# Pooled attention into gated attention experts: single PSUM banks, all loads cast on the way, and one written order for four engines

## The chip, the core and the metric

The kernel runs on one core of a Trainium2 chip. The metric is the device time of one execution in microseconds, as the median of several runs. A core has five instruction streams that matter here: TensorE (PE; its weight loads are listed apart as PEld), VectorE (DVE), ScalarE (ACT), GpSimd (POOL) and the sync engine (SP), which only issues transfers. They run at the same time, each in its own fixed order, and wait for each other through semaphores.

## The reference

There are 8 batches of 576 rows, 8 heads of 64. Stage A is attention against pooled keys and values: each run of 8 rows of k and of v is averaged, so 576 queries see 72 keys per head. The result x (576 x 512) goes into stage B, four causal attention experts of width 64, of which each row uses its best two, weighted by a softmax over their gates:

```python
k_p = k.reshape(B, H, Sp, pool, D).mean(axis=3)
v_p = v.reshape(B, H, Sp, pool, D).mean(axis=3)
attn = softmax(q @ k_p.T / sqrt(D));  x = attn @ v_p
...
topk = np.argpartition(-(x @ w_gate), 2)[..., :2]
for e in range(E):
    a = softmax(causal((x @ wq[e]) @ (x @ wk[e]).T / sqrt(Hd)))
    ye = a @ (x @ wv[e]) @ wo[e]
    out += (weight of e where e is in topk) * ye
```

(The softmax and causal mask are shortened here.)

## The kernel before, in words

Work is cut into units, each a few matmuls and what takes their result out of PSUM. One letter names a unit and a number its batch, so `N3:5` is unit N, index 3, of batch 5.

- `L` loads one chunk of k, q or v (three, five and three chunks a batch) by a GpSimd transfer that casts fp32 to bf16 (line 105). Four raw buffers of each kind turn round, so loads run up to three batches ahead.
- `Pk`, `Pv` pool k and v by matmuls with a small averaging matrix (line 199). ACT takes k out, DVE takes v out.
- `Pt` transposes the pooled k, `Q` transposes two heads of q (line 236), both copied out by DVE.
- `E` makes A's scores of two heads (line 252) and their exponentials on ACT (line 259). The scores of two heads share a double bank of 2 x 512, and each ACTIVATE covers half of the queries of both heads.
- `N` multiplies them with the pooled v of one head (line 268). A column of ones in v gives the sum; DVE takes its reciprocal (276) and multiplies (277).
- `X` transposes x (288), copied out by DVE (293).
- `q`, `k` project for a pair of experts, half of the rows at a time (361); ACT copies all of them out (368).
- `v` projects v of all four experts and the gate logits for 128 rows (303). With the fifth block DVE computes the gates, eleven small steps in one run (`gates`, lines 323 to 348).
- `s` makes B's scores for a pair of experts (387), exponentials on ACT (397), and zeroes the diagonal blocks' upper half on GpSimd (404).
- `o` multiplies them with v (417, one expert, two parts), and DVE scales by sum and gate (427 to 432). `T` transposes that (442), `y` multiplies with wo (455), and DVE (even blocks) or ACT (odd blocks) copies out before the store (467, 465).

The order on TensorE and GpSimd is the string SEQ. The order on DVE and ACT is made by a scheduler from its own costs. PSUM holds eight banks: the pool `p2` has two slots of two banks for scores, and `p1` four slots of one bank for everything else. A slot is used again in turn, so a new tile waits until the tile so many places before it has been read.

At the start batch 0 and the weights come uncast through SP (lines 113 to 131) into staging tiles, and DVE casts them (114, 136 to 148). One-element copies on GpSimd (lines 150 to 154) hold the loads of batch 1 back until a chunk of batch 0's v has arrived.

Of the kernel before, what the change touches and what calls it, by code (L numbers as in the profile page):

```python
# [8 lines left out]
FP32 = mybir.dt.float32  # L9
# [10 lines left out]
def kernel(  # L20
# [12 lines left out]
    nc = tc.nc  # L33
# [15 lines left out]
    NRAW = 4  # L49

# [4 lines left out]
    p2 = ctx.enter_context(tc.tile_pool(name="p2", bufs=2, space=bass.MemoryType.PSUM))  # L55
    p1 = ctx.enter_context(tc.tile_pool(name="p1", bufs=4, space=bass.MemoryType.PSUM))
    apool = ctx.enter_context(tc.tile_pool(name="apool", bufs=2))
    qtp = ctx.enter_context(tc.tile_pool(name="qtp", bufs=4))
    xtmp = ctx.enter_context(tc.tile_pool(name="xtmp", bufs=2))
    osp = ctx.enter_context(tc.tile_pool(name="osp", bufs=2))  # L60
    ofp = ctx.enter_context(tc.tile_pool(name="ofp", bufs=4))
    gtp = ctx.enter_context(tc.tile_pool(name="gtp", bufs=2))
    stp = ctx.enter_context(tc.tile_pool(name="stp", bufs=1))

    ident = const.tile([128, 128], BF16, name="ident")
    make_identity(nc, ident[:])

    KR = 96
    SPP = 96
    pool4 = const.tile([KR, 32], BF16, name="pool4")  # L70
    nc.gpsimd.memset(pool4[:], 1.0 / POOLW)
    nc.gpsimd.affine_select(
        out=pool4[:], in_=pool4[:], compare_op=ISGE, fill=0.0, base=0,
        pattern=[[-4, 32]], channel_multiplier=1,
    )
    nc.gpsimd.affine_select(
        out=pool4[:], in_=pool4[:], compare_op=ISGE, fill=0.0, base=3,
        pattern=[[4, 32]], channel_multiplier=-1,
    )

    qraws, kraws, vraws = [], [], []
    for i in range(NRAW):
        qraws.append(const.tile([128, NTC, H, D], BF16, name=f"qraw{i}"))
        kraws.append(const.tile([KR, 3, H, 2, D], BF16, name=f"kraw{i}"))
        vraws.append(const.tile([KR, 3, H, 2, D], BF16, name=f"vraw{i}"))
        nc.gpsimd.memset(qraws[i][64:128, NTC - 1, :, :], 0.0)

    def chunk(kind: str, b: int, c: int, dst):
        if kind == "q":
            n = min(128, S - 128 * c)  # L90
            return dst[0:n, c, :, :], q[b, :, 128 * c : 128 * c + n, :].rearrange("h p d -> p h d")
        return (
            dst[:, c, :, :, :].rearrange("p h t d -> p h (t d)"),
            (k if kind == "k" else v)[b, :, 2 * KR * c : 2 * KR * (c + 1), :].rearrange(
                "h (p t) d -> p h (t d)", t=2
            ),
        )

    CHUNKS = [("k", c) for c in range(3)] + [("q", c) for c in range(NTC)] + [("v", c) for c in range(3)]
    RAWS = {"q": qraws, "k": kraws, "v": vraws}  # L100

    def load_cast(b: int, i: int):
        kind, c = CHUNKS[i]
        dst, src = chunk(kind, b, c, RAWS[kind][b % NRAW])
        nc.gpsimd.dma_start(out=dst, in_=src)  # L105

    stage = {}
    for kind, c in CHUNKS:
        if c == 0:
            shape = [128, NTC, H, D] if kind == "q" else [KR, 3, H, 2, D]  # L110
            stage[kind] = stp.tile(shape, FP32, name=f"st_{kind}", tag=f"st_{kind}")
        dst, src = chunk(kind, 0, c, stage[kind])
        nc.sync.dma_start(out=dst, in_=src)  # L113
        nc.vector.tensor_copy(out=chunk(kind, 0, c, RAWS[kind][0])[0], in_=dst)  # L114

    wst = {}
    for nm, src, tag in (("q", moe_wq, "st_k"), ("k", moe_wk, "st_q"), ("v", moe_wv, "st_v")):
        wst[nm] = stp.tile([128, E, NFC, HD], FP32, name=f"wst_{nm}", tag=tag)
        nc.sync.dma_start(
            out=wst[nm][:].rearrange("p e fc d -> p (e fc) d"),  # L120
            in_=src.rearrange("e (fc p) d -> p (e fc) d", p=128),
        )
    wst["g"] = stp.tile([128, NFC, E], FP32, name="wst_g")
    nc.sync.dma_start(
        out=wst["g"][:], in_=moe_w_gate[:, :].rearrange("(fc p) e -> p fc e", p=128)
    )
    wst["o"] = stp.tile([128, NEP, DM], FP32, name="wst_o")
    nc.sync.dma_start(
        out=wst["o"][:],
        in_=moe_wo.rearrange("e d n -> (e d) n").rearrange("(ep p) n -> p ep n", p=128),  # L130
    )
    wqk = {}
    for ep in range(NEP):
        for nm in ("q", "k"):
            wqk[nm, ep] = const.tile([128, NFC, 128], BF16, name=f"w{nm}p{ep}")
            nc.vector.tensor_copy(
                out=wqk[nm, ep][:].rearrange("p fc (e d) -> p e fc d", e=2),
                in_=wst[nm][:, 2 * ep : 2 * ep + 2, :, :],
            )
    wvg = const.tile([128, NFC, VG], BF16, name="wvg")  # L140
    nc.vector.tensor_copy(
        out=wvg[:, :, 0 : E * HD].rearrange("p fc (e d) -> p e fc d", e=E), in_=wst["v"][:]
    )
    nc.vector.tensor_copy(out=wvg[:, :, E * HD : VG], in_=wst["g"][:])
    wop = []
    for ep in range(NEP):
        wop.append(const.tile([128, DM], BF16, name=f"wop{ep}"))
        nc.vector.tensor_copy(out=wop[ep][:], in_=wst["o"][:, ep, :])

    for i in range(NTC):  # L150
        nc.gpsimd.tensor_copy(out=qraws[1][0:1, i, 0, 0:1], in_=stage["v"][0:1, 1, 0, 0, 0:1])
    for r in (kraws[1], vraws[1]):
        for i in range(3):
            nc.gpsimd.tensor_copy(out=r[0:1, i, 0, 0, 0:1], in_=stage["v"][0:1, 1, 0, 0, 0:1])

    NETA, NETB, NKT, NVA, NXT = 4, 3, 4, 2, 2
    etas = [const.tile([SPP, 2, SPAD], BF16, name=f"eta{i}") for i in range(NETA)]
    for t in etas:
        nc.vector.memset(t[:, :, S:SPAD], 1.0)
    EOFF = [0, 576, 1024, 1344, 1536]  # L160
    ECOLS = 1664
    etbs = [const.tile([128, 2, ECOLS], BF16, name=f"etb{i}") for i in range(NETB)]
    for t in etbs:
        nc.vector.memset(t[:, :, 1600:ECOLS], 1.0)
    kts = [const.tile([128, SPAD], BF16, name=f"kt{i}") for i in range(NKT)]
    for t in kts:
        nc.vector.memset(t[:, S:SPAD], 0.0)
    vaugs = [const.tile([128, NTC, E, HD + 1], BF16, name=f"vaug{i}") for i in range(NVA)]
    for t in vaugs:
        nc.vector.memset(t[:, :, :, HD : HD + 1], 1.0)  # L170
    ones = const.tile([KR, 1], BF16, name="ones")
    nc.vector.memset(ones[:], POOLW / 4.0)
    one_ps = p1.tile([SPP, 1], FP32, name="one_ps", tag="p1")
    for c in range(3):
        nc.tensor.matmul(
            out=one_ps[32 * c : 32 * c + 32, :], lhsT=pool4[:, :], rhs=ones[:], start=True, stop=True
        )
    vps = [const.tile([SPP, H, D + 1], BF16, name=f"vpaug{i}") for i in range(2)]
    for t in vps:
        for h in range(H):  # L180
            nc.vector.tensor_copy(out=t[:, h, D : D + 1], in_=one_ps[:])
    xTbufs = [const.tile([128, NFC, SPAD], BF16, name=f"xT{i}") for i in range(NXT)]
    oTbufs = [const.tile([128, SPAD], BF16, name=f"oT{i}") for i in range(4)]
    for t in xTbufs:
        nc.vector.memset(t[:, :, S:SPAD], 0.0)
    for t in oTbufs:
        nc.vector.memset(t[:, S:SPAD], 0.0)
    turn = {"eta": 0, "etb": 0, "kt": 0, "oT": 0}

    def take(kind, ring):  # L190
        t = ring[turn[kind] % len(ring)]
        turn[kind] += 1
        return t
# [51 lines left out]
    def scores_a(st, hp: int):  # L245
        eta = st["eta", hp] = take("eta", etas)
        qT, kpT = st["qT", hp], st["kpT"]
        for c0, c1 in ((0, S // 2), (S // 2, S)):
            s_ps = p2.tile([SPP, 2, 512], FP32, name="sA_ps", tag="p2")
            for hh in range(2):  # L250
                r0 = hh * D
                nc.tensor.matmul(  # L252
                    out=s_ps[:, hh, 0 : c1 - c0],
                    lhsT=kpT[r0 : r0 + D, hp, :],
                    rhs=qT[r0 : r0 + D, c0:c1],
                    start=True,
                    stop=True,
                )
            nc.scalar.activation(  # L259
                out=eta[:, :, c0:c1], in_=s_ps[:, :, 0 : c1 - c0], func=EXP, scale=ATT_EXP_SCALE  # L260
            )

    def av_a(st, h: int):
        eta, vpaug, x_tm = st["eta", h // 2], st["vp"], st["x_tm"]
        hh = h % 2
        o_ps = p1.tile([128, NTC, D + 1], FP32, name="oA_ps", tag="p1")
        for c in range(NTC):
            nc.tensor.matmul(  # L268
                out=o_ps[:, c, :],
                lhsT=eta[:, hh, c * 128 : (c + 1) * 128],  # L270
# [24 lines left out]
    def v_proj(st, tc_: int):  # L295
# [19 lines left out]
        if tc_ == NTC - 1:  # L315
            st["G"] = gates(L)

# [242 lines left out]
```

The softmax here doesn't subtract the row's maximum and nothing guards it: scores larger than these inputs give would overflow.

## Time and profile before

| what | before |
|---|---|
| time, median of 4 runs | 208.4 us (208.3 to 208.54) |
| span of the profiled execution | 206.8 us |
| PE busy | 176.1 us, 2133 matmuls |
| DVE busy | 157.4 us, 567 instructions |
| ACT busy | 123.7 us, 225 instructions |
| POOL busy | 96.7 us, 181 instructions |
| first projection starts | 34.8 us |
| transfers | 87404 packets, 73.5% of 16 engines' span from GpSimd, 25.1% from SP |

Busy time is the union of an engine's instructions, and matmuls are pipelined, so a full TensorE need not be at its peak. Slices are fortieths of the span, in tenths. A group of instructions has a line, an engine, output and inputs with shapes, a count, the busy time, the mean of one, and the idle time before it with what ended it. The chain follows the work back from the last instruction to what released each step.

### The profile page before, as it was taken

To read this page: it belongs to the slowest core of one execution; us is meant where nothing else is said; L and a number is where in the kernel's file an instruction comes from. 1 tells how busy PE (TensorE), PEld (TensorE's weight loads), DVE (VectorE), ACT (ScalarE), POOL (GpSimd) and SP (SyncE) were. 2 spreads that over 40 slices of the span, in tenths; PEclk is the share of its full clock that TensorE was granted. 3 is DMA by queue.
4 is the path that set the end of the run, shared out by engine and by line. 5 is a ranking of instruction groups with operands and counts; after the bars stand their busy time and mean duration, and the time that the engine had idled before them with its cause. 6 is when DMAs were issued, how large, how long until landed. Compare 5 with 4: busy or idle time off the path is not lost.

```text
span 206.8 us, 5590 instructions
## 1 busy us (share of the span) xinstructions
PE 176.1 (85%) x2133; PEld 117.0 (57%) x2147; DVE 157.4 (76%) x567; ACT 123.7 (60%) x225; POOL 96.7 (47%) x181
## 2 busy tenths in 40 slices
PE   0126779999999899989999999999998999999762
PEld 0001446665676577646865776667755776785530
DVE  4645685749977987998989869997998779968642
ACT  2000442599358956765788667685877597747611
POOL 6009849785973493572845673635113012303300
PEclk9999999999999999999999999999999999999955
DMA  6999999999899969699599997997222102204315
GB/s 167 273 274 200 184 224 169 173 172 136 59 156 196 149 87 164 103 179 202 47 146 169 131 148 78 249 122 66 28 101 79 54 0 103 82 3 152 129 44 187
DMA packets 87404, 27.84 MB, mean 135 GB/s; under 512 B 77904, under 2 KB 82512, under 8 KB 87376
## 3 DMA queue, kind: packets, MB, share of 16 engines
q0 software_dynamic: 65744, 12.39, 73.5%
q1 hardware_dynamic: 21632, 15.09, 25.1%
q8 instruction: 17, 0.28, 0.5%
q14 instruction: 11, 0.09, 0.2%
HBM read 30.42 MB, written 9.44 MB: 193 GB/s over the span
## 4 chain that ended last, share of the span: by engine, by line
PE 61%; DVE 12%; ACT 12%; issue 5%; SPq 4%; DMA 3%; POOL 0%; ACTq 0%; DVEq 0%; POOLq 0%
PE qp_ps L361 7%; PE vg_ps L303 7%; PE oB_ps L417 6%; PE y_ps L455 6%; PE kp_ps L361 5%; PE sA_ps L252 5%; PE qT_ps L236 4%; PE xT_ps L288 4%; SPq L113 4%; ACT etb L397 4%; ACT eta L259 4%; PE sB_ps L387 4%; PE oA_ps L268 4%; DMA st_v<-in_v_dram 3%; DVE x_tm L277 3%
## 5 line engine op out<-in xcount | busy, mean ns | idle before, releaser
L404 POOL TENSOR_SCALAR_AFFINE_SELECT etb<-etb 128x256 bf16<-128x256 bf16 (+1 forms) x80 | 29.2, 386 | 81.1 <-ACT etb L397 76.7
L397 ACT ACTIVATE etb<-sB_ps 128x1024 bf16<-128x1024 f32 x64 | 50.0, 846 | 9.1 <-PE sB_ps L387 8.7
L259 ACT ACTIVATE eta<-sA_ps 96x576 bf16<-96x576 f32 x64 | 38.2, 644 | 12.6 <-PE sA_ps L252 11.9
L105 POOL DMA_DIRECT2D qraw<-in_q_dram x35 | 30.6, 876 | 2.1 <-DMA kraw<-in_k_dram 1.6
L277 DVE TENSOR_TENSOR x_tm<-oA_ps,rz 128x320 bf16<-128x320 f32 x64 | 30.6, 485 | 1.1
L303 PE MATMUL vg_ps<-wvg,xT 128*128 128x260 bf16 x160 | 23.7, 274 | 0.2
L268 PE MATMUL oA_ps<-vpaug,eta 96*128 96x65 bf16 x320 | 21.6, 200 | 1.9 <-ACT eta L259 1.5
L455 PE MATMUL y_ps<-wop,oT 128*128 128x512 bf16 x66 | 22.1, 415 | 1.2 <-DVE xT L293 0.7
L236 PE MATMUL qT_ps<-ident,qraw 128*128 128x128 bf16 x160 | 15.9, 233 | 8.0 <-DVE qraw L114 7.9
L417 PE MATMUL oB_ps<-vaug,etb 128*128 128x65 bf16 x480 | 21.8, 193 | 0.9 <-POOL etb L404 0.7
L268 PEld LDWEIGHTS <-eta 96*128 96x128 bf16 x320 | 16.2, 100 | 10.4 <-issue 4.0
L361 PE MATMUL qp_ps<-xT,wqp 128*128 128x288 bf16 x128 | 21.6, 291 | 0.2
L417 PEld LDWEIGHTS <-etb 128*128 128x128 bf16 x480 | 18.7, 97 | 4.9 <-issue 2.5
L467 DVE COPY ofin<-y_ps 128x512 f32<-128x512 f32 (+1 forms) x24 | 16.3, 683 | 6.7 <-PE y_ps L455 4.3
L368 ACT CAST qTB<-qp_ps 128x288 bf16<-128x288 f32 x32 | 12.8, 401 | 13.6 <-PE qp_ps L361 13.1
L361 PE MATMUL kp_ps<-xT,wkp 128*128 128x288 bf16 x128 | 20.9, 286 | 0.1
L310 DVE CAST vaug<-vg_ps 128x256 bf16<-128x256 f32 x40 | 16.8, 422 | 5.3 <-PE vg_ps L303 4.8
L387 PE MATMUL sB_ps<-qTB,kt 64*128 64x512 bf16 (+2 forms) x192 | 18.2, 277 | 2.7 <-ACT etb L397 1.9
L368 ACT CAST kt<-kp_ps 128x288 bf16<-128x288 f32 x32 | 12.9, 402 | 9.9 <-PE kp_ps L361 9.5
L105 POOL DMA_DIRECT2D vraw<-in_v_dram x21 | 16.9, 811 | 3.3 <-DMA kraw<-in_k_dram 2.2
L211 ACT CAST kp<-kp_ps 96x512 bf16<-96x512 f32 x8 | 4.7, 584 | 22.6 <-PE kp_ps L199 22.6
L242 DVE COPY qT<-qT_ps 128x576 bf16<-128x576 bf16 x32 | 14.2, 452 | 4.6 <-PE qT_ps L236 4.5
(72 smaller groups left out, 280.9 us busy)
## 6 DMA issues: line engine op xcount, KB each, us to landing
out_dram<-ofin SPq DMA_DIRECT2D x32, 256.0 KB, 2.2
kraw<-in_k_dram POOLq DMA_DIRECT2D x21, 192.0 KB, 6.7
vraw<-in_v_dram POOLq DMA_DIRECT2D x21, 192.0 KB, 5.8
qraw<-in_q_dram POOLq DMA_DIRECT2D x28, 128.0 KB, 6.1
st_k<-in_k_dram SPq DMA_DIRECT2D x3, 384.0 KB, 4.6
st_v<-in_v_dram SPq DMA_DIRECT2D x3, 384.0 KB, 5.9
st_q<-in_q_dram SPq DMA_DIRECT2D x4, 256.0 KB, 4.9
out_dram<-ofin SPq DMA_DIRECT2D x8, 128.0 KB, 2.7
```

The costliest lines, as they stand in the source:

```text
L105: nc.gpsimd.dma_start(out=dst, in_=src)
L259: nc.scalar.activation(out=eta[:, :, c0:c1], in_=s_ps[:, :, 0 : c1 - c0], func=EXP, scale=ATT_EXP_SCALE)
L268: nc.tensor.matmul(out=o_ps[:, c, :], lhsT=eta[:, hh, c * 128 : (c + 1) * 128], rhs=vpaug[:, h, :], start=True, stop=True,)
L277: nc.vector.tensor_tensor(out=x_tm[:, :, h * D : (h + 1) * D], in0=o_ps[:, :, 0:D], in1=rz[:].to_broadcast([128, NTC, D]), op=MULT,)
L303: nc.tensor.matmul(out=vg_ps[:], lhsT=xT[:, fc, tc_ * 128 : (tc_ + 1) * 128], rhs=wvg[:, fc, :], start=(fc == 0), stop=(fc == NFC - 1),)
L361: nc.tensor.matmul(out=p_ps[:], lhsT=wqk[nm, ep][:, fc, :], rhs=xT[:, fc, cols], start=(fc == 0), stop=(fc == NFC - 1),)
L368: nc.scalar.copy(out=st[nm, ep][:, cols], in_=p_ps[:])
L387: nc.tensor.matmul(out=s_ps[:, e, off : off + c1 - c0], lhsT=kT[r0 : r0 + HD, kc * 128 : (kc + 1) * 128], rhs=qT[r0 : r0 + HD, c0:c1], sta ...
L397: nc.scalar.activation(out=et[:, :, eo : eo + off], in_=s_ps[:, :, 0:off], func=EXP, scale=MOE_EXP_SCALE)
L404: nc.gpsimd.affine_select(out=blk, in_=blk, pattern=[[0, 2], [1, n]], compare_op=ISGE, fill=0.0, base=0, channel_multiplier=-1,)
L417: nc.tensor.matmul(out=o_ps[:, qc, :], lhsT=et[:, eloc, col : col + 128], rhs=vaug[:, kc, e, :], start=(kc == 0), stop=(kc == qc),)
L455: nc.tensor.matmul(out=y_ps[:], lhsT=st["oT", ep][:, qc * 128 : (qc + 1) * 128], rhs=wop[ep][:], start=(ep == 0), stop=(ep == NEP - 1),)
```

## The change

The change rewrites how units use PSUM, how data come in, and who sets the order.

1. All PSUM tiles take one bank, from one pool of eight slots. Scores of two heads or two experts go to two tiles, with one ACTIVATE for each. The last 64 queries of all pairs are collected into a unit of their own (`E4`, `s2x`), so the others are 512 columns wide. N takes two heads, o two experts.
2. Batch 0 and the weights are loaded by casting GpSimd transfers too. Staging tiles, casts and the holding copies go. The constants are made after the first 13 loads, the weights come as 15 loads after load 30. Memsets of the padding go to DVE.
3. SEQ now sets the order on TensorE, ACT, DVE and GpSimd. A letter `d` sends a projection's or an output's copy to DVE, otherwise ACT makes it: of 64 projection copies 31 go to DVE, of 40 output copies 10.
4. The gates become nine units (`g0` to `g8`) that other work can stand between. DVE takes reciprocals and products of N and o in pairs.
5. There are three xT buffers in place of two, eight slots for qT and for output tiles in place of four. The scores' results are kept per batch, two of each.
6. The new order puts stage A of batches 0 and 1 and much of 2 before the first projection, and works on two or three batches at a time up to the end.

The purpose is to have more PSUM tiles under way, to share the copies between ACT and DVE, to keep dependent small steps apart, and to free DVE of the casts.

```diff
-    p2 = ctx.enter_context(tc.tile_pool(name="p2", bufs=2, space=bass.MemoryType.PSUM))
-    p1 = ctx.enter_context(tc.tile_pool(name="p1", bufs=4, space=bass.MemoryType.PSUM))
+    p1 = ctx.enter_context(tc.tile_pool(name="p1", bufs=8, space=bass.MemoryType.PSUM))
...
-        nc.sync.dma_start(out=dst, in_=src)
-        nc.vector.tensor_copy(out=chunk(kind, 0, c, RAWS[kind][0])[0], in_=dst)
...
+    def load_weights():
+        for nm, src in (("q", moe_wq), ("k", moe_wk)):
+            for ep in range(NEP):
+                for e in range(2):
+                    nc.gpsimd.dma_start(
+                        out=wqk[nm, ep][:, :, e * HD : (e + 1) * HD],
+                        in_=src[2 * ep + e].rearrange("(fc p) d -> p fc d", p=128),
+                    )
...
     def scores_a(st, hp: int):
-        for c0, c1 in ((0, S // 2), (S // 2, S)):
-            s_ps = p2.tile([SPP, 2, 512], FP32, name="sA_ps", tag="p2")
...
-            nc.scalar.activation(
-                out=eta[:, :, c0:c1], in_=s_ps[:, :, 0 : c1 - c0], func=EXP, scale=ATT_EXP_SCALE
-            )
+        s_ps = [p1.tile([SPP, 512], FP32, name="sA_ps", tag="p1") for _ in range(2)]
+        tail = hp == NHP
...
+                nc.scalar.activation(
+                    out=eta[:, hp, hh, 0:512], in_=s_ps[hh][:], func=EXP, scale=ATT_EXP_SCALE
+                )
...
+        for hh in range(2):
+            nc.vector.reciprocal(out=rz[:, hh], in_=o_ps[hh][:, :, D : D + 1])
+        for hh in range(2):
+            h = 2 * hp + hh
+            nc.vector.tensor_tensor(
...
-        nc.scalar.copy(out=st[nm, ep][:, cols], in_=p_ps[:])
+        copy(out=st[nm, ep][:, cols], in_=p_ps[:])
...
-    with tc.manual_schedule(engines={ENG.Pool, ENG.PE}):
+    with tc.manual_schedule(engines={ENG.PE, ENG.Activation, ENG.DVE, ENG.Pool}):
...
+            copy = nc.vector.tensor_copy if on_dve else nc.scalar.copy
```

The first rows of the new order, up to the first projection, and its last:

```diff
+        L1:0 L9:0 L2:0 L7:0 L6:0 L4:0 M:0 L8:0 L5:0 L0:0 L3:0 L10:0 L8:1 L0:2 I:0 Q0:0
+        Pk:0 Pv:0 Pt:0 L2:1 L0:1 Q1:0 Q2:0 L1:1 Q3:0 L3:1 E0:0 L6:1 L4:1 E4:0 E2:0 L7:1
+        E1:0 N0:0 Pk:1 N2:0 L5:1 N1:0 X0:0 Pt:1 E3:0 X1:0 Q3:1 Q1:1 L9:1 Q0:1 L10:1 Q2:1
+        N3:0 E1:1 Pv:1 E4:1 L1:2 L2:2 E2:1 L5:2 L3:2 X3:0 N1:1 E0:1 L6:2 N2:1 X1:1 L7:2
+        L4:2 N0:1 Pk:2 E3:1 W:0 X2:0 L8:2 L9:2 Q1:2 Pt:2 Q2:2 Q0:2 L10:2 N3:1 E1:2 L0:3
+        E0:2 L1:3 E2:2 c0:0 Q3:2 X2:1 X0:1 L2:3 X3:1 L3:3 q00:0 q10d:0 L4:3 q11d:0 q01d:0 c1:0
...
+        y4:4 y1:7 o00:6 o01:6 y4:7 y0:7 T1:6 y2:7 T0:6 y3d:7 y2:6 y0d:6 y1:6 y3d:6 y4:6
```

Here `I` makes the constants, `M` the memsets, `W` the 15 weight loads; `c` does nothing.

## The prediction

> **What bounds the kernel now.** I read the page's engine shares and slices first, then stages of the span, then the chain in order of time, then groups of instructions by shape.
>
> ```profile
> PE 176.1 (85%) x2133; PEld 117.0 (57%) x2147; DVE 157.4 (76%) x567; ACT 123.7 (60%) x225; POOL 96.7 (47%) x181
> ...
> PE   0126779999999899989999999999998999999762
> ...
> PE 61%; DVE 12%; ACT 12%; issue 5%; SPq 4%; DMA 3%; POOL 0%; ACTq 0%; DVEq 0%; POOLq 0%
> ```
>
> TensorE is the engine with the most work, full from about 36 us to 190 us, and ramps before that. Stages (span from:to, length, busy us of PE, weight loads, DVE, ACT, POOL, clock, DMA share, GB/s):
>
> ```profile
> 0.00:10.00 10.00, 0.55 (x5) 0.29 (x5) 5.66 (x42) 1.28 (x1) 3.17 (x13) 1.00 0.92 219
> 10.00:20.00 10.00, 4.26 (x21) 1.34 (x21) 4.55 (x9) 0.00 (x0) 4.67 (x14) 1.00 1.09 244
> 20.00:30.00 10.00, 7.57 (x64) 4.12 (x60) 7.01 (x21) 4.14 (x7) 7.23 (x9) 1.00 1.68 203
> ...
> 40.00:190.00 150.00, 144.29 (x1867) 99.97 (x1880) 125.45 (x455) 108.28 (x200) 70.71 (x128) 1.00 0.95 116
> 190.00:206.80 16.80, 9.79 (x98) 5.09 (x97) 8.03 (x27) 5.99 (x11) 2.85 (x8) 0.71 0.37 126
> ```
>
> The middle 150 us have TensorE at 96%, DVE at 84% and ACT at 72%. The losses stand at both ends. The chain shows what makes the ends long (start, length, what):
>
> ```profile
> 10.16 7.05 DMA st_v<-in_v_dram
> ...
> 33.20 0.97 PE kp_ps L199 x6
> 34.82 0.96 PE qp_ps L361 x4
> ...
> 73.25 0.54 PE kp_ps L199 x6
> ...
> 79.58 0.49 PE qp_ps L361 x4
> ...
> 199.40 3.63 PE y_ps L455 x8
> ```
>
> Batch 0's last v chunk arrives only at 17.2 us. The same six pooling matmuls take 0.97 us at 33 us and 0.54 us later, so TensorE runs at about half speed until some 35 us, and again at the end (0.45 us for each y matmul against about 0.22 in the middle).
>
> **A price list of TensorE.** From start to start in the crowded stretch 100 to 112 us: pooling 0.54, five transposes 0.29, four projection matmuls 0.49, four v matmuls 0.45, two y matmuls 0.43, 15 of the o matmuls 0.46, five N matmuls 0.17, scores 0.48 (A) and 1.40 (B, a pair of experts). A batch makes 20.4 us, eight make 163.3. About 8.3 us of this stand before the first projection, which starts at 34.8; the other 155.0 take until 206.8, that is 172.0. So 17.0 us are lost after the ramp. About 6.0 us of work are left at 191.2, and 15.6 us of time: 9.6 are lost in the tail and 7.4 (4.7%) in the middle.
>
> **What the Trainium skill says.** "TensorE: Matmul & The Clock Gate", section "What's actually happening": the array runs at half clock until a window of about 3.4 us of activity has passed, and falls back when idle. The doubled durations above agree; the clock row of the page does not show the slow start. "ScalarE: Activation LUTs", section "What ACT_TABLE_LOAD costs": an ACTIVATE costs a fixed part plus 0.833 ns per element, and neighbours overlap. The rows below agree (388 ns for 448 more elements, 0.866). "DMA: Bandwidth & Descriptors", section "SWDGE vs HWDGE vs iDMA": a cast on the way needs GpSimd to make the descriptors. The trace has it as 0.78 to 0.90 us of POOL per load. "VectorE: DVE Perf Modes", section "The DRAIN you can't avoid": an instruction that is held waits for the pipe to empty; the gate chain below agrees.
>
> ```profile
> L397 ACT ACTIVATE etb<-sB_ps 128x1024 bf16<-128x1024 f32 x48 | 47.3, 1032 | 9.1 <-PE sB_ps L387 8.7
> L259 ACT ACTIVATE eta<-sA_ps 96x576 bf16<-96x576 f32 x64 | 38.2, 644 | 12.6 <-PE sA_ps L252 11.9 <-PE oA_ps L268 0.7
> ...
> L105 POOL DMA_DIRECT2D kraw<-in_k_dram x21 | 16.3, 783 | 0.3
> ...
> L310 DVE CAST vaug<-vg_ps 128x256 bf16<-128x256 f32 x40 | 16.8, 422 | 5.3 <-PE vg_ps L303 4.8
> ...
> L465 ACT COPY ofin<-y_ps 128x512 f32<-128x512 f32 x16 | 9.5, 594 | 10.3 <-PE y_ps L455 5.4 <-PE oT_ps L442 4.8
> ```
>
> **The change, part by part.** *TensorE's work*: 16 score matmuls per batch in A and 24 in B before and after, the same columns in other cuts (4608 and 6400). Sum unchanged at 163.3 us.
>
> *ACT.* One bank per ACTIVATE, heads apart. Net of overlap, 576 elements cost 38.2/64 = 0.597 us and 1024 cost 47.3/48 = 0.985, so 512 cost about 0.54 and 256 about 0.32. A: 64 x 0.54 + 16 x 0.32 = 39.7 against 38.2, +1.5. B: 96 x 0.54 + 16 x 0.25 = 55.8 against 51.9, +3.9. Y copies rise from 16 to 30: 14 x 0.594 = +8.3. Of 64 projection copies 31 leave: 31 x 0.40 = -12.4. Total +1.3: about 125 us.
>
> *DVE.* The casts of batch 0 and of the weights go (11 and 8 instructions, -10), the 16 copies of ones become two (-1), y copies fall from 24 to 10 (-9.5), and 31 projection copies come: the nearest row is 422 ns for 256 columns, so 0.45 each, +14 (bounds 12 and 15). Memsets moved from POOL +1. About 152 us against 157.4.
>
> *Dependent DVE steps.* Before, the eleven gate steps stood in one run, each behind its predecessor:
>
> ```profile
> 88.90 0.39 DVE L324 TENSOR_TENSOR lo<-L 128x10 f32<-128x10 f32 x1
> ...
> 91.17 0.38 PE L455 MATMUL y_ps<-wop,oT 128*128 128x512 bf16 x1 [0.66 <-DVE xT L293]
> ```
>
> That run filled 88.8 to 92.1 us, and TensorE stood for 0.66 us because DVE came late to a transposed x whose PSUM slot the y matmul needed. Nine separate steps with other work between, and N in pairs (two reciprocals, then two products), remove such stops: between 0 and 1 us per batch. But all four orders are now fixed by hand, and an order that does not fit the chip's times stops an engine with work behind it. PSUM goes from four single and two double slots to eight singles, in rotation; a score, N or o unit takes two, so some five units are in flight against four plus two. I take 5 us for the middle loss in place of 7.4 (bounds 1 and 16).
>
> *The start.* All batch 0 loads go through POOL. In its queue 13 loads stand before the four selects that make identity and pooling matrix: from 0.9 us, 13 x 0.83 = 10.8, plus 4 x 0.25 to 0.3, so TensorE starts at about 13 to 14 us (before: 8.5). The eleventh load is issued at about 9.5 and lands 5 to 6 us later (median of these loads 5.8 to 6.7), about 15 us against 17.2; no cast follows. So the first A exponential comes near 20.5 us against 22.8.
>
> Then comes the larger re-ordering: A of batches 0 and 1 and half of 2 go before the first projection. TensorE's sum to there is 17.0 us in place of 8.3. DVE's is 22.5 us of single durations, 20 with the overlap seen before. From 14 us, with a few us at half clock and DVE as the bound of this stretch, the first projection comes at about 39 us. The weights are loads 31 to 45 of POOL's queue: at the 0.89 us per load that 17 to 45 us showed (32 loads in 28.5 us), the wq of pair 0 is issued by 30 and lands by 36, wk by 41, wv by 45. TensorE wants them at 39, 43 and about 47. They just fit; this hides behind A. The first causal select stands behind load 56, about 52 us; what reads it (o of batch 0) is 23 us of TensorE work after the first projection, near 63. Hidden.
>
> So at 39 us 17.0 us of work are done, where before 34.8 us had done 8.3, which puts before at about 12 at 39 us: a lead of 4 to 5 us.
>
> *The tail.* Outputs of batches 4 to 7 are kept for the end, so y work fills the waits of the last chain. After the last o matmul: six DVE steps 1.4, transposes 0.5, copy 0.5, five y 2.2 to 4.3, copy 0.7, landing 2.5: about 8 to 10 us, beside which lie 4 us of TensorE work. I take 7 lost against 9.6.
>
> *Sum.* 39 + (163.3 - 17.0) + 5 + 7 = 197.3 us of span. The measured time is 1.6 over the span (208.4 against 206.8): 198.9, say 199.
>
> **Rivals.** *The weights bind* (0.10): loads slow to 1.1 us, wv lands at 55; TensorE stands some 6 to 8 us: about 206. For it: only POOL issues, landing up to 10.8 us. Against: 0.89 kept up while DMA slices showed 9. *The middle runs nearly full* (0.20): loss of 1 and warm tail of 5: 193. For it: DVE is lighter and its chains are broken up. Against: ACT at 125 still comes in bursts. *Fixed orders stop engines* (0.13, slower): before, two of the four orders came from the scheduler; if the loss in the middle is 11% of 139 us = 15.5 and the first projection slips to 42, 39 + 3 + 146.3 + 15.5 + 7 + 1.6 = 212. For it: in several rows of the new order ACT has more work than TensorE (6.3 against 5.2 us). Against: the neighbours have less, and eight slots carry that. The forecast has the rest, 0.57.
>
> **How the numbers follow.** Range 191.5 to 209: below 193 only the best of the second case, above 209 most of the last. Faster: the forecast, the second case and nearly all of the first: 0.84. Slower 0.13; same 0.03.
>
> **What would show it.** TensorE begins near 14 us, the first projection near 39, and its busy time in the first 10 us is about nil; DVE near 152 and ACT near 125 us; the longest waits of TensorE behind DVE gone; last store within 10 us of the last o matmul. I am wrong if wq, wk or wv loads release TensorE, if TensorE falls back to half clock in the A stretch, or if waits for ACT grow in the middle.

## The result and the profile after

The changed kernel takes 184.63 us (median, 184.1 to 186.95) against 208.32 us: ratio 0.8877, 95% interval 0.8846 to 0.8907. It is 14 us faster than forecast and lies below the range. From here on "before" and "changed" name the two kernels; every ratio of an experiment is to before, so 0.8877 is the mark to compare with.

The page of the changed kernel, its busy times, TensorE's slices and the engines' shares of the chain:

```profile
PE 157.3 (86%) x2136; PEld 111.5 (61%) x2147; DVE 144.2 (79%) x555; ACT 121.8 (66%) x272; POOL 110.7 (60%) x183
...
PE   0007888799999999999999999999999999999950
...
PE 64%; POOL 10%; DMA 7%; ACT 7%; DVE 6%; issue 2%; POOLq 0%; ACTq 0%; DVEq 0%
```

The stages, in the columns used in the prediction (span, length, busy us of PE, weight loads, DVE, ACT, POOL, clock, DMA share, GB/s):

```profile
15.00:20.00 5.00, 5.00 (x40) 3.01 (x42) 2.72 (x6) 0.58 (x1) 4.96 (x7) 1.00 1.83 179
20.00:40.00 20.00, 17.39 (x244) 11.78 (x241) 16.93 (x55) 13.70 (x29) 17.89 (x25) 1.00 2.02 141
40.00:163.50 123.50, 121.72 (x1672) 88.63 (x1680) 107.86 (x421) 94.95 (x220) 70.67 (x122) 1.00 1.06 122
163.50:183.50 20.00, 12.95 (x186) 8.01 (x188) 12.72 (x50) 11.31 (x22) 3.47 (x9) 0.92 0.63 220
```

TensorE is busy for 98.6% of the middle (96% before). Yet its busy time over the whole span fell by 18.8 us for the same matmuls. Part of this is the start at half clock, which ended at 20.0 us in place of 36.5; the rest is waiting that had counted as "busy", and this view could not say how much. TensorE's timeline at the start (start, length, what, and in brackets the idle time and what ended it):

```profile
14.99 0.71 PE L208 MATMUL qT_ps<-ident,qraw 128*128 128x128 bf16 x5 [2.29 <-DMA qraw<-in_q_dram]
15.63 1.04 PE L171 MATMUL kp_ps<-kraw,pool 96*32 96x512 bf16 x6
...
22.01 0.61 PE L171 MATMUL kp_ps<-kraw,pool 96*32 96x512 bf16 x6
...
37.62 0.65 PE L355 MATMUL qp_ps<-xT,wqp 128*128 128x288 bf16 x4
```

The same six pooling matmuls take 1.04 us at 15.6 us and 0.61 at 22. The trace's clock records put full speed from 20.0 us; before it was 36.5 us. The waits of TensorE between 40 and 165 us, complete (total, times, longest):

```profile
PE vg_ps L288 <- ACT etb L394: 0.3, 1, 0.3
PE y_ps L465 <- ACT etb L394: 0.3, 1, 0.3
```

In 125 us there are two waits for another engine in this view, of 0.3 us each. The chain's end (start, length, what):

```profile
174.87 2.35 PE y_ps L465 x10
...
177.28 0.58 ACT ofin L474
```

The last output's store lands at 182.5 us, and the span ends at 183.5.

**Where the 23.3 us came from.** I added up the columns of all matmuls by time, at 2.4 columns per ns (pooling's column thirds counted as a third), as a yardstick of work done; score pairs that run side by side are counted in full, so it is no utilisation. (The rate is from the changed kernel's trace: a next pair of score matmuls starts 187 ns after one of 448 columns and 133 after one of 320.) At 40 us the changed kernel has done 17.6 us; before gets there at 47.3. At 190.0 us before has done 143.5; the changed kernel gets there at 168.4. For equal work:

| part | before, us | changed, us | gain | forecast |
|---|---|---|---|---|
| start, to 17.6 us of work | 47.3 | 40.0 | 7.3 | 4 to 5 |
| middle, to 143.5 | 142.7 | 128.4 | 14.3 | 2.4 |
| end | 16.8 | 15.1 | 1.7 | 2.6 |

Some matmul records are missing in both traces, which can move up to 1 us between the last two rows. The middle is the surprise. My theory after this comparison: spaced order and eight-slot ring need each other; together they let TensorE run ahead of ACT and DVE. The rivals: DVE's looser chains alone, the fixed order on ACT and DVE alone, the copies' sharing, or the start's loads and clock.

### The profile page after: what moved, and what is told of

Its sections match the earlier page's. It is cut to its first block, busy times and chain, and to the rows that moved or that the text cites. A ratio compares the mean times of both kernels' runs of the same rounds, so it can differ in the third digit from the quotient of the medians.

```text
span 183.5 us, 5524 instructions
## 1 busy us (share of the span) xinstructions
PE 157.3 (86%) x2136; PEld 111.5 (61%) x2147; DVE 144.2 (79%) x555; ACT 121.8 (66%) x272; POOL 110.7 (60%) x183
## 4 chain that ended last, share of the span: by engine, by line
PE 64%; POOL 10%; DMA 7%; ACT 7%; DVE 6%; issue 2%; POOLq 0%; ACTq 0%; DVEq 0%
PE kp_ps L355 9%; PE qp_ps L355 8%; PE vg_ps L288 8%; PE oB_ps L423 7%; PE y_ps L465 7%; PE sB_ps L376 5%; PE xT_ps L273 4%; POOL qraw L142 4%; PE sA_ps L224 4%; DMA kraw<-in_k_dram 4%; DMA qraw<-in_q_dram 4%; PE oA_ps L250 4%; PE qT_ps L208 3%; POOL kraw L142 3%; ACT etb L394 3%; PE oT_ps L452 2%
## 5 line engine op out<-in xcount | busy, mean ns | idle before, releaser
L407 POOL TENSOR_SCALAR_AFFINE_SELECT etb<-etb 128x256 bf16<-128x256 bf16 x64 | 25.8, 420 | 51.7 <-ACT etb L394 51.7
L394 ACT ACTIVATE etb<-sB_ps 128x512 bf16<-128x512 f32 x96 | 50.5, 624 | 1.7 <-PE sB_ps L376 1.7
L239 ACT ACTIVATE eta<-sA_ps 96x512 bf16<-96x512 f32 x64 | 33.7, 614 | 7.1 <-PE sA_ps L224 7.0
L142 POOL DMA_DIRECT2D qraw<-in_q_dram x40 | 34.2, 881 | 1.0 <-DMA qraw<-in_q_dram 0.6
L474 ACT COPY ofin<-y_ps 128x512 f32<-128x512 f32 (+1 forms) x30 | 16.9, 599 | 8.3 <-PE y_ps L465 3.2
L355 PE MATMUL kp_ps<-xT,wkp 128*128 128x288 bf16 x128 | 19.8, 286 | 0.0
L355 PE MATMUL qp_ps<-xT,wqp 128*128 128x288 bf16 x128 | 19.8, 286 | 0.0
L142 POOL DMA_DIRECT2D kraw<-in_k_dram x24 | 18.9, 807 | 1.2 <-POOLq L560 0.8
L423 PE MATMUL oB_ps<-vaug,etb 128*128 128x65 bf16 x480 | 17.9, 193 | 0.2
L288 PEld LDWEIGHTS <-xT 128*128 128x128 bf16 x160 | 14.5, 97 | 4.5 <-issue 1.8
L376 PE MATMUL sB_ps<-qTB,kt 64*128 64x64 bf16 (+4 forms) x192 | 16.8, 276 | 0.3
L183 ACT CAST kp<-kp_ps 96x512 bf16<-96x512 f32 x8 | 4.8, 601 | 17.6 <-PE kp_ps L171 17.6
L250 PEld LDWEIGHTS <-eta 96*128 96x128 bf16 x320 | 13.5, 98 | 4.7 <-ACT eta L239 1.5
L250 PE MATMUL oA_ps<-vpaug,eta 96*128 96x65 bf16 x320 | 15.5, 194 | 1.0 <-ACT eta L233 0.5
```

Source lines behind the costliest of these rows:

```text
L239: nc.scalar.activation(out=eta[:, hp, hh, 0:512], in_=s_ps[hh][:], func=EXP, scale=ATT_EXP_SCALE)
L250: nc.tensor.matmul(out=o_ps[hh][:, c, :], lhsT=eta[:, c * 128 : (c + 1) * 128], rhs=vpaug[:, 2 * hp + hh, :], start=True, stop=True,)
L288: nc.tensor.matmul(out=vg_ps[:], lhsT=xT[:, fc, tc_ * 128 : (tc_ + 1) * 128], rhs=wvg[:, fc, :], start=(fc == 0), stop=(fc == NFC - 1),)
L355: nc.tensor.matmul(out=p_ps[:], lhsT=wqk[nm, ep][:, fc, :], rhs=xT[:, fc, cols], start=(fc == 0), stop=(fc == NFC - 1),)
L376: nc.tensor.matmul(out=s_ps[e][:, off : off + c1 - c0], lhsT=st["k", i][r0 : r0 + HD, kc * 128 : (kc + 1) * 128], rhs=st["q", i][r0 : r0 + ...
L394: nc.scalar.activation(out=et[:, ep, e, eo : eo + off], in_=s_ps[e][:, 0:off], func=EXP, scale=MOE_EXP_SCALE)
```

## Experiments

**How many PSUM slots.** From the changed kernel, the ring alone:

```diff
-    p1 = ctx.enter_context(tc.tile_pool(name="p1", bufs=8, space=bass.MemoryType.PSUM))
+    p1 = ctx.enter_context(tc.tile_pool(name="p1", bufs=6, space=bass.MemoryType.PSUM))
```

> The changed kernel with six PSUM slots in place of eight, nothing else. In the changed kernel the middle of the span (40 us to 20 us before the end) runs with no loss on TensorE, where before it lost about 14 us. Slot theory: it is the number of tiles under way that gives this; with six the middle loses again, 192 us or more. Order theory (the written order alone keeps producer and consumer far enough apart): six are nearly enough, 185 to 188 us.

202.4 us, 0.9714 (0.9646 to 0.9782). The same edit with 7:

> The changed kernel with seven PSUM slots. Six took 202.4 us and eight 184.6. If the loss falls evenly with each slot, about 193; if the order needs just about six to seven, below 188; if it was made for eight turns of the ring, near 200.

191.36 us, 0.9147 (0.9106 to 0.9189). Third, eight slots in two fixed halves: scores in a pool `ps` of four, all else in `p1` of four (edits here and below are shortened).

```diff
-p1, bufs=8
+p1, bufs=4
+ps, bufs=4      # sA_ps and sB_ps only
```

> The changed kernel with its eight single PSUM banks divided as before: four for scores, four for all else. The number of banks is the same. If a shared ring lets TensorE run further ahead, 192 or more, near the 202 of six slots; if only the count of banks matters, within 2 us of 184.6.

222.78 us, 1.0676 (1.0626 to 1.0727): slower than before, and far slower than the forecast, "near the 202 of six slots". The middles, in the stage columns, six slots, then seven, then four and four:

```profile
40.00:181.50 141.50, 134.28 (x1694) 92.56 (x1692) 111.16 (x428) 97.19 (x222) 71.23 (x123) 1.00 0.93 108
```

```profile
40.00:169.90 129.90, 126.38 (x1670) 89.75 (x1677) 109.03 (x421) 95.15 (x219) 70.23 (x121) 1.00 1.01 115
```

```profile
40.00:201.60 161.60, 141.68 (x1697) 93.51 (x1702) 112.50 (x433) 98.79 (x224) 71.63 (x124) 1.00 0.82 96
```

Nearly the same matmuls fill 121.7 us of PE busy time with eight slots, 126.4 with seven, 134.3 with six, 141.7 with two halves. The added "busy" time is waiting, inside the modelled matmuls. The first slot taken away costs 6.7 us, the second 11. In the split, what is long is not a named data wait but the score weight loads standing for nothing that the profile shows (waits of weight loads: total, times, longest; in the changed kernel this line is L376 with 4.1 us in 14 times):

```profile
PEld L377 <- issue: 17.1, 41, 0.8
```

A score matmul waiting for its slot would look so, but the view doesn't name it. The traces can: match each PSUM tile with the one whose slot it takes over (slots in the order of their release; some 7% of the matches don't fit), and ask how often its first matmul starts within 40 to 60 ns after the last reader of that older tile has ended. Of some 530 tiles that is so for 17 with eight slots, 48 with seven, 88 with six and 113 with two halves. So TensorE waits for slots, and the more so the fewer there are. The written order assumes that any unit may take any free slot. An order made for two halves wasn't tried.

**The order.** The old order of units carried over into the changed structure (Q units moved ahead of the first N and followed by `E4`, the new units placed at the earliest point that their inputs allow, gates in one run, all projection copies on ACT, output copies in turn, weights loaded after batch 1), all four engines written:

```diff
-SEQ = the new order
+SEQ = the order of before, in units of the changed kernel
```

> The old order of units in the structure of the changed kernel: eight single slots, casting loads for all, four engines in the written order, projections copied by ACT alone and outputs in turn as before; the remaining q transposes of a batch are drawn ahead of its first N, because the collected scores of the last 64 queries need them, and the weights are loaded after batch 1. Order theory: most of the gain goes, 200 to 208 us. Slot or small-step theory: the middle still runs nearly full, 190 to 196 us.

232.64 us, 1.1166 (1.1077 to 1.1255). The same, with ACT and DVE left to the scheduler:

```diff
-    with tc.manual_schedule(engines={ENG.PE, ENG.Activation, ENG.DVE, ENG.Pool}):
+    with tc.manual_schedule(engines={ENG.PE, ENG.Pool}):
```

> The old order in the structure of the changed kernel as in the run that took 232.6 us, but with ACT and DVE ordered by the scheduler. If the forced order on these two engines made it slow, 205 us or less. If the order on TensorE does not fit the ring of eight single slots, 220 or more.

225.61 us, 1.0793 (1.0747 to 1.0839). So the structure with the old order is a loss of 17 to 24 us, more than the forecast of 200 to 208 for the first run allowed, and a hand-fixed order on ACT and DVE is only 7 of it. Part of the loss is the clock, which fell back to half in both runs: in the first at 50.5 to 53.9, 91.4 to 94.9 and 214.3 to 224.6 us. Waits of TensorE in the first of the two, from 40 to 210 us:

```profile
PE xT_ps L273 <- DVE x_tm L262: 6.9, 9, 2.3
PE oA_ps L250 <- ACT eta L233: 6.1, 7, 1.6
```

The second line is the collected last-64-query unit: N of every pair now waits for the one exponential that comes last. How much of the loss is this requirement and how much the old spacing isn't separated by a run. It is no lack of slots: by the same match only 7 tiles of the first run start right after their slot came free. The reverse, the new order with the scheduler on ACT and DVE (the edit just shown, in the changed kernel):

> The changed kernel with the orders of ACT and DVE left to the scheduler again, TensorE and GpSimd as written. If it was the scheduler's order on these two engines that cost the middle before, 192 us or more. If the order on TensorE, the slots or the small DVE steps matter, it stays within 3 us of 184.6.

188.96 us, 0.9058 (0.8977 to 0.9139): the written order on ACT and DVE is worth 4 us, which meets neither of the two forecasts. Between this run and the old order with the same scheduler lie 37 us. In them the order of TensorE and GpSimd, the gate units and the sharing of copies differ together, so they are no measure of TensorE's order alone.

**Dependent DVE steps.** Gates in one run (`g0` to `g8` in a row), then N and o with each head's or expert's reciprocal followed at once by its product (the diff shows N; o is edited in the same way), then both:

```diff
-... g0:1 (other units) g1:1 (other units) g2:1 ...
+... g0:1 g1:1 g2:1 g3:1 g4:1 g5:1 g6:1 g7:1 g8:1 ...
```

> The changed kernel with the nine gate steps of a batch in one run again, where the first step stood; N and o stay in pairs. With both undone DVE was busy for 156.8 us in place of 144.2 and the time was 199.7. If the gate runs are the cost, most of the 15 us show here, 195 or more, and DVE is busy for over 152 us; if it is the turn of reciprocal and product in 64 heads and 32 experts, under 188.

195.74 us, 0.9436 (0.9374 to 0.9498).

```diff
         for hh in range(2):
             nc.vector.reciprocal(out=rz[:, hh], in_=o_ps[hh][:, :, D : D + 1])
-        for hh in range(2):
             h = 2 * hp + hh
...
```

> The changed kernel with reciprocal and product in turn for each head and expert; gates stay in nine separate steps. If the pairs are what matters, 193 or more and DVE busy for over 150 us; if the gate runs, under 188 and DVE busy under 147 us.

191.27 us, 0.9208 (0.9136 to 0.9279), between the two forecasts. Both:

> The changed kernel with the gate steps in one run again and with reciprocal and product in turn for each head and expert. Theory of the dependent DVE steps: each of eight gate runs stops TensorE for up to 1 us and each pair costs 0.1 us more of DVE, so 190 us or more. Order or slot theory: TensorE has tiles enough to go on with, under 187 us.

199.69 us, 0.9566 (0.9488 to 0.9645). The costs nearly add: 11.1 and 6.6 make 17.7, together 15.1. DVE is busy for 149.1, 153.5 and 156.8 us in the three runs, against 144.2. The gate run adds less busy time than the pairs undone, and costs more time; so DVE's total doesn't decide. That it matters when DVE is late is argued, not shown. Of DVE's timeline with the gates in a run:

```profile
64.83 0.16 DVE L310 TENSOR_TENSOR hi<-L 128x10 f32<-128x10 f32 x1
64.91 0.17 DVE L310 TENSOR_TENSOR lo<-L 128x10 f32<-128x10 f32 x1
...
65.56 0.32 DVE L320 TENSOR_TENSOR m<-s,s 128x5 f32<-128x5 f32 x1
65.90 0.34 DVE L324 TENSOR_TENSOR msk<-L,m 128x20 f32<-128x20 f32 x1
66.34 0.18 DVE L328 TENSOR_TENSOR W<-Ex,msk 128x20 f32<-128x20 f32 x1
66.56 0.17 DVE L330 TENSOR_TENSOR d<-W 128x10 f32<-128x10 f32 x1
66.76 0.17 DVE L334 SCALAR_TENSOR_TENSOR den<-d 128x5 f32<-128x5 f32 x1
66.96 0.19 DVE L339 RECIPROCAL rden<-den 128x5 f32<-128x5 f32 x1
```

and three steps of a batch in the changed kernel:

```profile
65.54 0.15 DVE L316 TENSOR_TENSOR s<-lo 128x5 f32<-128x5 f32 x1
...
68.52 0.16 DVE L320 TENSOR_TENSOR m<-s,s 128x5 f32<-128x5 f32 x1
69.62 0.17 DVE L324 TENSOR_TENSOR msk<-L,m 128x20 f32<-128x20 f32 x1
```

The steps themselves are not longer in a run: over all eight batches their median is 0.17 us in both kernels, and single long ones, of 0.3 to 0.46, occur in both. What differs is the distance. A step that reads the result of the one before it starts about 0.20 us after it, once that one has ended (66.56, 66.76, 66.96; later behind a long one, as at 65.90 and 66.34); a step that doesn't follows after 0.08 (64.83, 64.91). With other work between, DVE does that work meanwhile. Time in which DVE has nothing but a gate step is 15.6 us with the gates in a run and 9.3 in the changed kernel, which makes 6.3 of the 11.1 us.

But in before it is 9.4. There the scheduler had already put other work ahead of 42 of the 88 gate steps (40 in the changed kernel, 8 with the gates in a run). So the nine gate units keep a hand-fixed order from losing 11 us; against before, the runs show no gain from them.

For the pairs, the groups (count | busy, mean ns | idle before, releaser) of the changed kernel:

```profile
L262 DVE TENSOR_TENSOR x_tm<-oA_ps,rz 128x320 bf16<-128x320 f32 x64 | 28.2, 482 | 0.0
L259 DVE RECIPROCAL rz<-oA_ps 128x5 f32<-128x5 f32 x64 | 8.9, 175 | 2.2 <-PE oA_ps L250 2.0
```

and with the pairs undone:

```profile
L261 DVE TENSOR_TENSOR x_tm<-oA_ps,rz 128x320 bf16<-128x320 f32 x64 | 31.5, 492 | 2.2
L259 DVE RECIPROCAL rz<-oA_ps 128x5 f32<-128x5 f32 x64 | 11.8, 184 | 1.9 <-PE oA_ps L250 1.8
```

The mean of one hardly moves, but neighbours overlap less: both groups together keep DVE busy for 35.1 us in pairs and 40.1 in turn (41.7 before), and o's three steps for 22.0 and 26.5 (25.8 before). A gate run also holds DVE back until ACT's exponential of the gates is there; this part isn't separated.

**The sharing of copies.** Projection copies all on ACT, output copies with an even number on DVE, units where they stood:

```diff
-q10d:0 q11d:0 q01d:0 ... y4:7 y0:7 ...
+q10:0 q11:0 q01:0 ... y4d:7 y0d:7 ...
```

> The changed kernel with the old shares of the copies: all 64 projection copies on ACT, the outputs of even blocks on DVE. By sums DVE gets 14 us less and 10 us more, ACT 12 more and 8 less, so neither engine's total changes by over 5 us. If only totals count, within 3 us of 184.6; if each copy stands on the engine that is free at that moment, 190 or more.

189.94 us, 0.9156 (0.9097 to 0.9214). DVE's busy time is 140.1 us, 4 less than in the changed kernel, and ACT's 125.0, 3 more. Totals so close can hardly make 5 us; that they come from where the copies stand is argued from this, not shown. The time lies at the edge of what was forecast for that case.

**The start.** Before, with batch 0 loaded by casting GpSimd transfers, its staging and casts gone:

```diff
-        (staged loads on SP, tensor_copy casts, holding copies)
+        for i in range(len(CHUNKS)):
+            load_cast(0, i)
```

> The kernel before with one part of the change: batch 0 comes by casting GpSimd loads, without staging tiles, casts and the copies that held batch 1 back; the weights still come through SP. Theory that the way of loading sets the start: first scores some 2 us earlier and 205 to 206.5 us in all. Theory that the gain of the start comes from the order of the units (work of A in front while the weights come): no more than 1 us, 207 to 209.

213.28 us, 1.0264 (1.0194 to 1.0333): a loss that neither theory expected, with 7.2 us of work done by 40 us against 10.8. In the changed structure, with the same way of loading, the old order has done 13.5 by then (first run of the order above) and the new one 17.6. So casting loads alone lose, the structure with the old order gains 2.7 us of work by 40 us, and the new order, with A of further batches to fill the start, another 4.1.

Then the changed kernel with q loaded first, the constants behind two loads and all Q units ahead of `Pk`:

```diff
-        L1:0 L9:0 L2:0 L7:0 L6:0 L4:0 M:0 ... I:0 Q0:0 Pk:0 Pv:0 Pt:0 ...
+        L6:0 L4:0 I:0 L5:0 L3:0 L7:0 ... Q0:0 Q1:0 Q2:0 Q3:0 Pk:0 Pt:0 Pv:0 ...
```

> The changed kernel with another head of the order alone: q of batch 0 is loaded first, the constants are made after two loads, and all four q transposes stand ahead of the pooling of k. If the wait for the last q chunk and the constants (until 15.0 us) sets the start, TensorE begins near 10 us, is at full speed earlier, and the time falls by 2 to 3 us. If the arrival of k and v sets it, no change.

186.67 us, 0.8963 (0.8925 to 0.9001): 1% slower, though TensorE starts 5 us sooner:

```profile
9.67 2.42 PE L208 MATMUL qT_ps<-ident,qraw 128*128 128x128 bf16 x20 [5.61 <-DMA qraw<-in_q_dram]
14.36 1.04 PE L171 MATMUL kp_ps<-kraw,pool 96*32 96x512 bf16 x6 [2.28 <-DMA kraw<-in_k_dram]
23.22 1.04 PE L171 MATMUL kp_ps<-kraw,pool 96*32 96x512 bf16 x5 [0.33 <-DMA kraw<-in_k_dram]
```

It starts with gaps, the pooling at 23.2 us is still at half speed (1.04 us), full clock comes at 29.5, and 15.8 us of work are done by 40 us in place of 17.6. In this one run the later start was the better one; the order of the loads changed with it, so it doesn't show the gaps to be the cause.

Is it the clock as such? Matmuls 128x512 on a constant tile, whose result nobody reads, were put at the start: 12 of them behind `Q0:0` of before, and 40 ahead of everything in the changed kernel.

```diff
+    def H(n):  # n matmuls 128x512 on a constant tile, nothing reads them
```

> The kernel before with twelve matmuls of 512 columns on a constant tile, whose result nobody reads, between the first q transposes and the pooling of v, where TensorE waits for v from 12.7 to 18 us. Clock theory: TensorE reaches full speed by about 20 us in place of 36.5 and the A stage of batches 0 and 1 goes faster, 203 to 206 us. If transfers and the small steps set the pace there, no gain, 208 to 209; it may also fall back to half clock, and then nothing is gained.

> The changed kernel with 40 such matmuls before its first work, in the time in which TensorE waits for the first data. Clock theory: full speed from the first pooling on at 15 us, 1 to 2 us faster, 182.5 to 183.5. If DVE and the loads set the pace after 20 us, the same 184.6.

Before with filling: 208.69 us, 0.9979 (0.9954 to 1.0005), no difference. The clock rose at 19.5 us and fell back at 26.3, as the clock column shows (1.00 is full):

```profile
20.00:30.00 10.00, 6.92 (x75) 3.63 (x72) 8.13 (x24) 4.73 (x9) 8.37 (x10) 0.82 1.61 210
30.00:40.00 10.00, 8.89 (x67) 5.75 (x67) 4.78 (x14) 2.53 (x7) 7.91 (x11) 0.50 2.06 171
```

This profile is of an execution of 211.2 us, so only its clock is read here. The changed kernel with filling: 184.39 us, 0.883 (0.8796 to 0.8865), overlapping the changed kernel's interval. The clock was full from 6.1 us, but real work began only at 15.07, and from 16.4 to 19.8 us the clock was at half again:

```profile
16.40:19.80 3.40, 3.25 (x34) 2.59 (x33) 2.38 (x5) 0.62 (x2) 3.40 (x5) 0.50 1.83 179
```

So little changed: the first pooling took 0.61 us in place of 1.04, and TensorE's work was some 0.7 us ahead at 22 us. Neither kernel got a full clock that lasted from its first work on, so what this is worth stays open in both.

**The end.** Kept outputs of batch 4 stored earlier, so that the last stores find the queues empty:

```diff
-        ... y0:4 y3:4 y2d:4 (in the last rows)
+        ... v1:7 y0d:4 ... s01:7 y3d:4 ... v3:7 y2d:4 ...
```

> The changed kernel with three outputs of batch 4 moved some 15 us ahead, into the stretch of 148 to 161 us that has no store, and copied by DVE. If the stores at the end are limited by how fast they can be written (the last lands 4.7 us after its copy, against 2.0 for one alone), 1 to 3 us faster. If these outputs are needed as filling for TensorE's waits in the tail, or the copies disturb DVE, slower.

186.01 us, 0.892 (0.8886 to 0.8955): no gain. Together with the early start:

> Both, the early start and the early stores: if each gains by itself the sum, 180 to 182; otherwise the sign of the one that loses.

187.7 us, 0.9002 (0.8972 to 0.9033). No version tried beats the changed kernel by more than the intervals.

## Why the prediction was wrong

**Right**: the direction and most of the signs. TensorE starts at 15.0 us (14 forecast), first projection at 37.6 (39), first A exponential at 20.2 (20.5), ACT 121.8 us (125); no weight load releases TensorE, and the wait for a late x is gone. The rival "the middle runs nearly full" was the nearer case, and still 8 us too slow. But the main gain came in the middle, 14.3 us where 2.4 was forecast.

**The step that failed: the price list of TensorE**, in its row "scores 0.48 (A) and 1.40 (B, a pair of experts)", and with it "a batch makes 20.4 us", "17.0 us are lost after the ramp" and "7.4 (4.7%) in the middle". The two matmuls of a score pair were priced as if one followed the other: 0.48 is what the 1152 columns of a unit of A take at 2.4 columns per ns; the 3200 columns of a pair of experts would take 1.33, and where 1.40 comes from the record doesn't say. The stretch of before that the list names, 100 to 112 us, shows less. From the start of a score unit to the start of what comes next it is 0.38 in A, and 0.54 and 0.35 for the two parts of a pair in B, 0.90 together:

```profile
99.86 0.45 PE L252 MATMUL sA_ps<-qT,kpT 64*96 64x288 bf16 x4
100.24 0.45 PE L236 MATMUL qT_ps<-ident,qraw 128*128 128x128 bf16 x5
...
104.38 0.61 PE L387 MATMUL sB_ps<-qTB,kt 64*128 64x512 bf16 x6
104.92 1.07 PE L303 MATMUL vg_ps<-wvg,xT 128*128 128x260 bf16 x8
...
108.47 0.42 PE L387 MATMUL sB_ps<-qTB,kt 64*128 64x320 bf16 x6
108.82 0.32 PE L268 MATMUL oA_ps<-vpaug,eta 96*128 96x65 bf16 x5
```

So a batch has 4 x 0.38 + 2 x 0.90 = 3.3 us of scores in place of 4.72, 82 ns for each of 40 matmuls, and the changed kernel has the same 82 ns. They can be that short because the two heads or the two experts of a pair take 64 rows each: in the traces of both kernels their starts lie 3 to 4 ns apart. The Trainium skill says so, "TensorEngine Tiling (Array Packing)", section "Key Properties": tiles operate independently, and different tiles can load weights and multiply in parallel. I had not used it.

With that one row mended the same sum reads so (us):

| term | forecast: before, changed | with scores at 82 ns: before, changed |
|---|---|---|
| first projection starts | 34.8, 39 | 34.8, 37.6 |
| work after it | 155.0, 146.3 | 144.1, 136.2 |
| lost after it | 17.0, 12 | 27.9, 9.7 |

(Left after the first projection are eight batches of B, and of A seven before and 5.6 in the changed kernel; each B is 0.83 shorter, each A 0.61.) The loss that stood there to be removed was 28 us, not 17: 11 us of waiting were booked as work that no change of order could take away. I had called a middle 95% full that was 88% full by the yardstick above (now 98%). Of the 14 us between forecast and measurement this row makes about 10. The first projection, 1.4 us sooner, the loss left over, 9.7 in place of 12, and a smaller difference of time and span (1.1 in place of 1.6) make the rest.

**"Dependent DVE steps: between 0 and 1 us per batch"** holds for the pairs, whose 6.6 us are 0.8 per batch. The 11.1 us of the gate run don't count against it, since before was not in that state: the reading "each behind its predecessor" was only partly right, and in the batch shown there other copies and products stand between the last gate steps. DVE fell by 13.2 us, to 144.2, not by 5.4. What was counted came out nearly as forecast (casts -9.3, output copies -8.7, projection copies +12.5); missing in the sum are the pairs of N and o, about 6.5 us where each moment is shared out evenly among the instructions that run in it, while the gates make 0.2. The page quoted for this, "VectorE: DVE Perf Modes", section "The DRAIN you can't avoid", states that the next instruction does not start until the pipe has emptied, and that one which is not held starts earlier. The distances above, 0.20 against 0.08 us, agree in kind; how much of them is the pipe and how much the wait for the result no run here shows.

**The start** gained 7.3 in place of 4 to 5: first projection 1.4 us sooner than forecast, and before had done 10.9 us of the list's work at 39 us, not 12. The clock rose after 5.00 of 5.00 us busy, and in nine runs that start like the changed kernel 3.4 to 6.1 us after the first matmul. This agrees with "TensorE: Matmul & The Clock Gate", section "What's actually happening", by which it takes a window of some 3.4 us of sustained activity; in before 75% busy from 20 to 30 us didn't raise it.

**"Fixed orders stop engines"**, the slower rival, is what the old order in the new structure does, 226 to 233 us. With the new order it didn't happen. That the new order needs the ring is shown: with seven and six slots it loses 7 and 18 us, and on two halves it is slower than before. The other way round, the old order gains nothing from the ring; it is seen waiting for data, and hardly ever for a slot. Which units of the new order matter most isn't shown.

## What to carry to other kernels

Check each row of a price list against the starts in the trace: matmuls that start together are not to be added one after the other, or waiting is booked as work. An engine that looks full may still wait inside its instructions (121.7 us busy became 141.7 here with the slots in two halves, for the same matmuls). Judge a ring of buffers and the order that fills it together, and in small steps, since a single slot was worth 7 to 11 us here. In an order fixed by hand, put other work between small dependent steps of VectorE: all in a row they cost 11 us. A start of TensorE that is 5 us sooner is no gain by itself; in the one run that tried it the kernel was 1% slower.

## What the hardware showed that was not expected

- Two matmuls with 64 rows each start 3 to 4 ns apart; 40 score matmuls per batch take 82 ns each from start to start, though their 11008 columns one after the other would make 115 (at 2.4 columns per ns).
- The clock falls back when TensorE's work is broken, but these runs give no threshold. In the old-order runs it fell at 50.5, 91.4 and 63.4 us, in the filled kernels at 16.4 and 26.3, with the gates in a run at 35.9. In the 3.4 us before each of these falls TensorE was busy for 1.3 to 2.1 us. Yet a stretch as idle in the old order, 1.1 us busy in the 3.4 us up to 49 us, brought no fall at once.
- The mean length of a VectorE instruction says little of its cost: 64 reciprocals and 64 products keep the engine busy for 35.1 us in pairs and 40.1 in turn, though the means hardly move (175 and 482 ns, 184 and 492).
